# A decay-attention and gated-convolution kernel on one core: decay from ln(a_re), two small first units, a column-tiled state product and a pinned order

## The chip, the core and the metric

The kernel runs on one core of a Trainium2 chip. A core has five engines that work side by side and wait for one another through semaphores: TensorE (PE in the profile; its weight loads are shown apart as PEld), VectorE (DVE), ScalarE (ACT), GpSimd (POOL) and SyncE (SP), which here issues every DMA. The metric is the device time of one execution in microseconds. Three executions of the kernel before are shown, with their median; the profile is of one more execution.

## What is computed

For each of 4 batches and 8 heads, a state of 48 x 48 complex numbers decays by a complex factor per row and step, takes in an outer product of k and v, and is read out with q. The outputs of the 8 heads, side by side (384 columns), then go through a gated convolution. The reference, cut:

```
mag = np.sqrt(a_re * a_re + a_im * a_im)
scale = np.minimum(mag, 0.999) / (mag + 1e-06)
a_re_n, a_im_n = (a_re * scale, a_im * scale)
for t in range(S):                                  # S = 768
    new_re = ar * S_re - ai * S_im                  # ar, ai: step t of a_re_n, a_im_n
    new_im = ar * S_im + ai * S_re
    S_re, S_im = (new_re + kv, new_im)              # kv: outer product of k[t], v[t]
    y[:, :, t] = np.einsum('bhd,bhde->bhe', q[:, :, t], S_re)
...
gate = 1.0 / (1.0 + np.exp(-gate_pre))              # gate_pre: 5 taps along the sequence
return (gate * (x @ w_val) @ w_out)                 # x: y with the heads side by side
```

All inputs but the three convolution weights are float32; those are float64 and are rebuilt as float32 from their 64-bit words on the core.

## The kernel before

The recurrence is turned into chunked attention. The running product of the decay factors has a logarithm (a running sum of log magnitudes) and an angle (a running sum of angles). k is multiplied by one over that product and q by the product, each as a cosine and a sine part, so a head has 96 rows (48 cosine, 48 sine). The sequence is cut into 6 chunks of 128 steps. A chunk's output is a masked score matrix times v plus q times the state left by the chunks before.

The work goes in units: (batch, first head, number of heads). There are seven units of 4 heads and, at the end, two of 2 heads. A unit passes through these stages; a letter names each in the string `ORDER`:

- A, X, R (lines 277 to 360): from `ar` and `ai` to the running sums. ACT squares both inputs (L277, L279), takes one logarithm of both squares (L294, 2304 elements a partition), two exponentials (L296, L298), and the arctangent (L312). Two further ACT passes, L315 and L321, are guards: a Relu whose sum is not zero where an input lies outside the range that the formulas hold for. DVE does L281, L301, L316, the running sums along a partition (L244) and the shifts that fold the angle into one turn. PE adds the sums of the partitions below (L251, tile `off`).
- S (L368, L372): sine and cosine. E (L377, L379): the two exponentials of the log magnitude, each with a sum that the guard tests too.
- B (L391, L394): `kx` and `qx` (the latter in the tile `trig`). `kx` is also written to DRAM (`kd`) and read back with the sequence along the partitions (`kn`).
- T (L436, L437): transposes on PE, one head at a time, copied by ACT out of PSUM into `kq` (96 partitions x 768 steps, for k and q).
- s, k (L459, L464): scores of a chunk on PE, masked by DVE into `sm`. t (L495, L500): the state product `kn` (stationary, 96 columns) times `v` (48 columns), summed up in PSUM and copied by ACT to `S_sb`. y (L477, L480, L481): the chunk's output. The outputs of odd heads go to PSUM partitions 64 and up, those of even heads to partition 0 and up.
- W: the convolution's weights. C (L521, L524): the taps on DVE. G (L532): the sigmoid on ACT. M (L539, L545, L571, L576): the two projections on PE, the gating product on DVE, the copy and the store of the output.

`ORDER` is walked letter by letter; each letter lets one stage issue its next step. A framework then places the instructions of an engine, with one restriction that the kernel adds (`in_turn`): ACT instructions that need a table set keep their order. Loads and stores on SP are issued as soon as their buffers are free by the program's own count.

A float32 matmul is two instructions on PE (a transpose is one), each with its weight load.

Of the kernel before, what the change touches and what calls it, by code (L numbers as in the profile page):

```python
# [10 lines left out]
F32 = mybir.dt.float32  # L11
U32 = mybir.dt.uint32
I64 = mybir.dt.int64
I32 = mybir.dt.int32
# [8 lines left out]
    "WWAWWWAWWWWAXXXXRRRRRRRRRWRRWRRWRRWRWRRWRSSEEBWBWWWWBWWWBTTTTWWWWWWWWWWsksyWksWAAAXXXWtXWyWksRWt"  # L23
    "WRyWksWRWtRWyWksRWtWRWykRWWtRWyCCRCCRtCRCARRARSSEEBBBAXXXXRRRRRRRRRRRRRRBTTTTtsksykskysktysSSEEB"
    "ktBBBysktyTtyTTtTACsksAkstCyAXXXXRRRRRRRRRRRRRCRSSEEBkstCAyCAkstCCCyAXXBCXCkstXyCCGMMMMMMMMMMMMM"
    "ktyBtyRRRRRRMRRRMBTTTTtstksyksytRkRMRRMsRSSyMtMkMMsyMtMkMMsCyEMtkCyAAAXXXEBBBBCXRRRRRRRRRRRRRRCT"
    "TCTSTttskskysytkytsksAytSEACCCCCCCCCCCksCAXyCGMMMMMMMMtEBMMBMMMXkyXXBRRRMRRMRRMRMRBTTTTstksykyst"
    "RMRRMRksMRSSEEyMtMAMksMyMtACCBMCCCCksAXytXkBytXBXRRRRRRRRRBTTTTsttkskysksyksRAAtAXXXXRyksRtRCCCy"
    "kCCRSSECCCCCCCGCCCCCCMMMMMMMMMMMMMtRREBBBRRRyRBTRRRRtRTtsksRMRMRMMMMMMMyCCCCCtkCMsMyktMMsyktsykt"
    "SSEEBBBBTsyktyTskstyyksytksytksytksytkytCCCCCCCCCCCCGCCCCCCGCCCCCCGMMMMMMMMMMMMMMMMMMMMMMMMMM"  # L30
)
TURN = 2.0 ** 24
# [3 lines left out]
SS_MIN = 0.25  # L36
RHO_MAX = 1.5
RE_MIN = 0.75
SS_MAX = 1.8
# [3 lines left out]
def kernel(  # L43
# [50 lines left out]
    last = [None]  # L94

    def in_turn(ins):

        if last[0] is not None:
            tc.add_manual_dep(
                ins.ins, last[0].name,  # L100
                mybir.DependencyInfo(mybir.DependencyClass.NoSync, mybir.DependencyReason.DATA),
                reason="one table set after the other",
            )
        last[0] = ins.ins
        return ins

    loaded = [None]

    def table_set(name):
        if loaded[0] != name:  # L110
            in_turn(nc.scalar.preload_act_table_set(name))  # L111
            loaded[0] = name
# [3 lines left out]
    def load(u, nm):  # L116
        b, h0, g = units[u]
        tl = tiles.setdefault(u, {"v": []})
        if nm == "v":
            for hn in range(2):  # L120
                vt = ld.tile([C, HN, g, D], F32, name="v_in", bufs=VB)
                for h in range(g):
                    nc.sync.dma_start(
                        out=vt[:, :, h, :],
                        in_=v[b, h0 + h, hn * HS:(hn + 1) * HS].rearrange("(n i) e -> i n e", i=C),
                    )
                tl["v"].append(vt)
        else:
            t = ld.tile([P, 2, g, JH, D], F32, name=f"{nm}_in", tag="in")
            for f in range(2):  # L130
                nc.sync.dma_start(  # L131
                    out=t[:, f].rearrange("p h j d -> p h (j d)"),
                    in_={"ar": a_re, "ai": a_im, "k": k, "q": q}[nm][b, h0:h0 + g, f * HS:(f + 1) * HS].rearrange(
                        "h (p j) d -> p h (j d)", j=JH
                    ),
                )
            tl[nm] = t
# [9 lines left out]
    load(0, "ai")  # L147

# [17 lines left out]
    b_tiny = const.tile([P, 1], F32, name="b_tiny")  # L166
    nc.gpsimd.memset(b_tiny, 2.0 ** -60)
    b_re = const.tile([P, 1], F32, name="b_re")
    nc.gpsimd.memset(b_re, RE_MIN)
    b_ss = const.tile([P, 1], F32, name="b_ss")  # L170
    nc.gpsimd.memset(b_ss, -math.log(SS_MAX))
    over = const.tile([P, 4, NU], F32, name="over")
    flag = const.tile([1, 1], I32, name="flag")
    junk = const.tile([P, G * D * J], BF16, name="junk")
# [4 lines left out]
    b_rho = const.tile([P, 1], F32, name="b_rho")  # L179
    nc.gpsimd.memset(b_rho, math.log(2.0 ** 31 / RHO_MAX))  # L180

# [72 lines left out]
    tmps = []  # L254

# [8 lines left out]
    def new_tmp(ne):  # L264
        tmps.append(False)
        return work.tile([P, 2, ne], F32, name="tmp", bufs=TMPB), len(tmps) - 1

    def tmp_free():
        return len(tmps) < TMPB or tmps[-TMPB]

    def prep_a(u):

        b, h0, g = units[u]
        tl = tiles[u]
        tl["main"] = work.tile([P, 2, JH, 2, g * D], F32, name="main", bufs=MAINB)
        main, mf, mj = views(u)
        nc.scalar.activation(mj[:, 1], jm(tl["ar"]), AF.Square)  # L277
        yield
        nc.scalar.activation(mj[:, 0], jm(tl["ai"]), AF.Square)  # L279
        yield  # L280
        nc.vector.scalar_tensor_tensor(  # L281
            out=mf[:, 0], in0=mf[:, 1], scalar=SS_MIN, in1=mf[:, 0], op0=ALU.max, op1=ALU.add
        )

    def prep_x(u):

        b, h0, g = units[u]
        tl = tiles[u]
        main, mf, mj = views(u)
        while not tmp_free():  # L290
            yield "wait"
# [663 lines left out]
```

## Time and profile before

| | us |
|---|---|
| median of three executions | 351.21 |
| lowest, highest of the three | 350.67, 356.26 |
| the profiled execution | 352.57 |
| its span, first to last instruction | 350.9 |
| PE busy / DVE busy / ACT busy in the span | 291.3 / 254.8 / 266.7 |
| DMA share of the 16 engines | 53.2% |

Busy time is the time that records of an engine cover. Matmul records overlap: one lasts about 0.25 us, the next may start 0.1 us after it. So how long PE needs for a row of matmuls is read from the distance of their starts, and not from their mean duration. The granted TensorE clock was 0.992 over the span.

### The profile page before, as it was taken

The page shows a single profiled execution, that of the slowest core. Times are in us where ns is not written, and L with a number is a line of the kernel's source. Part 1 is how long each engine was busy: PE and PEld are TensorE (multiplying, and loading weights), DVE is VectorE, ACT ScalarE, POOL GpSimd, SP SyncE. Part 2 cuts the span into 40 slices and gives each one's busy share as a digit, 9 for nine tenths or more (in the row PEclk, how much of TensorE's full clock was granted, in tenths as well). Part 3 has the DMA queues.
Part 4 walks back from the last instruction along what each step waited for, and adds up shares of the span by engine and source line. Part 5 has one row for each costly group of instructions (what it writes and reads, how often), then busy time and mean ns, then how long its engine had stood idle before and what let it go on. Part 6 is the DMA issues. An engine that isn't in the chain of part 4 may idle for free.

```text
span 350.9 us, 5801 instructions
## 1 busy us (share of the span) xinstructions
PE 291.3 (83%) x2154; PEld 221.7 (63%) x2154; DVE 254.8 (73%) x322; ACT 266.7 (76%) x454; POOL 2.5 (1%) x23
## 2 busy tenths in 40 slices
PE   0030298958988998999999999999999999999992
PEld 0020187748767775777887767777877775676551
DVE  0599987899685998788989786788479736356610
ACT  3958989998998989599879986998996375362201
POOL 2000000000000000000000000000000000000000
PEclk9999999989999999999999999999999999999998
DMA  7993781269579549745674576458410532520102
GB/s 230 370 243 67 241 239 61 61 196 356 124 214 256 148 117 296 220 110 174 194 210 102 151 218 212 95 186 275 92 39 2 153 102 92 164 48 21 62 32 67
DMA packets 84562, 54.73 MB, mean 156 GB/s; under 512 B 31024, under 2 KB 83760, under 8 KB 84528
## 3 DMA queue, kind: packets, MB, share of 16 engines
q1 hardware_dynamic: 84528, 54.30, 53.2%
q8 instruction: 19, 0.31, 0.4%
q14 instruction: 15, 0.12, 0.1%
HBM read 35.40 MB, written 14.16 MB: 141 GB/s over the span
## 4 chain that ended last, share of the span: by engine, by line
PE 67%; ACT 14%; DVE 6%; DMA 5%; SPq 3%; issue 2%; ACTq 0%
PE pv L539 13%; PE po L571 12%; PE pt L436 11%; PE sc L459 10%; PE S_ps L495 7%; PE y_ps L477 5%; PE y_ps L480 5%; PE off L251 3%; SPq L131 2%; DMA q_in<-in_q_dram 2%; ACT main L294 2%; ACT L111 2%; DMA kn<-kd 1%; ACT kq L437 1%; ACT junk L315 1%
## 5 line engine op out<-in xcount | busy, mean ns | idle before, releaser
L437 ACT COPY kq<-pt 96x384 f32<-96x384 f32 x128 | 55.8, 478 | 6.6 <-PE pt L436 6.1
L459 PE MATMUL sc<-kq 96*128 96x128 f32 x384 | 58.3, 282 | 2.0 <-DVE sm L464 2.0
L459 PEld LDWEIGHTS sc<-kq 96*128 96x128 f32 x384 | 50.6, 193 | 10.5 <-DVE sm L464 4.8
L539 PE MATMUL pv<-xT,wv_sb 128*128 128x384 f32 x144 | 54.8, 498 | 0.0
L571 PE MATMUL po<-wo_sb,z 128*128 128x384 f32 x144 | 51.7, 496 | 1.0 <-DVE z L545 1.0
L464 DVE TENSOR_TENSOR sm<-sc,mask 128x512 f32<-128x512 f32 (+1 forms) x54 | 34.0, 629 | 25.5 <-PE sc L459 15.7
L524 DVE SCALAR_TENSOR_TENSOR z<-xT,cw_sb,z 128x768 f32<-128x768 f32 (+1 forms) x60 | 50.6, 854 | 1.1
L436 PE MATMUL pt<-ident,kx 128*96 128x128 f32 x192 | 34.0, 288 | 15.1 <-DVE kx L394 12.2
L477 PE MATMUL y_ps<-kq,S_sb 96*48 96x128 f32 x320 | 39.8, 286 | 3.9 <-ACT y_sb L481 3.0
L480 PE MATMUL y_ps<-sm,v_in 128*48 128x128 f32 x384 | 42.1, 275 | 0.1
L436 PE MATMUL pt<-ident,trig 128*96 128x128 f32 x192 | 34.0, 286 | 6.4 <-DVE trig L394 5.0
L495 PE MATMUL S_ps<-v_in,kn 128*96 128x48 f32 x320 | 36.8, 247 | 1.3 <-DMA kn<-kd 0.8
L495 PEld LDWEIGHTS S_ps<-v_in,kn 128*96 128x96 f32 x320 | 34.0, 167 | 6.0 <-issue 4.5
L571 PEld LDWEIGHTS po<-wo_sb,z 128*128 128x128 f32 x144 | 25.7, 190 | 17.1 <-DVE z L545 2.3
L436 PEld LDWEIGHTS pt<-ident,kx 128*96 128x96 f32 x192 | 21.5, 132 | 21.7 <-DVE kx L394 12.9
L111 ACT ACT_TABLE_LOAD x25 | 32.1, 1283 | 1.2 <-PEq L939 0.8
L481 ACT COPY y_sb<-y_ps 112x256 f32<-112x256 f32 (+1 forms) x54 | 18.6, 345 | 18.2 <-PE y_ps L480 17.8
L436 PEld LDWEIGHTS pt<-ident,trig 128*96 128x96 f32 x192 | 21.7, 132 | 16.1 <-issue 6.9
L539 PEld LDWEIGHTS pv<-xT,wv_sb 128*128 128x128 f32 x144 | 24.4, 190 | 9.9 <-issue 0.9
L576 ACT COPY ot<-po 128x384 f32<-128x384 f32 x24 | 11.4, 478 | 24.1 <-PE po L571 23.8
L477 PEld LDWEIGHTS y_ps<-kq,S_sb 96*48 96x48 f32 x320 | 21.1, 122 | 13.6 <-ACT y_sb L481 5.6
L480 PEld LDWEIGHTS y_ps<-sm,v_in 128*48 128x48 f32 x384 | 27.4, 123 | 3.1 <-issue 0.7
(81 smaller groups left out, 394.5 us busy)
## 6 DMA issues: line engine op xcount, KB each, us to landing
kd<-kx SPq DMA_DIRECT2D x14, 576.0 KB, 3.5
kn<-kd SPq DMA_DIRECT2D x14, 576.0 KB, 4.7
v_in<-in_v_dram SPq DMA_DIRECT2D x64, 72.0 KB, 2.7
out_dram<-ot SPq DMA_DIRECT2D x24, 192.0 KB, 2.3
ar_in<-in_a_re_dram SPq DMA_DIRECT2D x14, 288.0 KB, 4.0
ai_in<-in_a_im_dram SPq DMA_DIRECT2D x14, 288.0 KB, 4.8
k_in<-in_k_dram SPq DMA_DIRECT2D x14, 288.0 KB, 3.4
q_in<-in_q_dram SPq DMA_DIRECT2D x14, 288.0 KB, 4.6
```

The lines of the kernel that those rows point to most:

```text
L111: in_turn(nc.scalar.preload_act_table_set(name))
L436: nc.tensor.transpose(pt[:C2, j, :], src[:, j, f, h, :], ident)
L437: nc.scalar.copy(tj[:, s, f], pt[:C2].rearrange("c j p -> c p j"))
L459: nc.tensor.matmul(sc[:, h, :], self.part(0, h, n), self.part(1, h, n), start=True, stop=True)
L464: nc.vector.tensor_tensor(out=sm, in0=sc[:, :g], in1=mask[:, None, :].to_broadcast([C, g, C]), op=ALU.mult)
L477: nc.tensor.matmul(o, self.S_sb[n - 1][:, h * D:(h + 1) * D], self.part(1, h, n), start=True, stop=False)
L480: nc.tensor.matmul(o, vt[:, h, :], sm[:, h, :], start=(n == 0), stop=True)
L481: nc.scalar.copy(self.y_sb[:112, :, (n % HN) * C:(n % HN + 1) * C], yp[:112, :g // 2 * C].rearrange("e (r t) -> e r t", t=C),)
L495: nc.tensor.matmul(self.S_ps[:C2, h * D:(h + 1) * D], kn[:, h, :], vt[:, h, :], start=(n == 0 and h == 0), stop=(n == NCH - 2), skip_group ...
L524: nc.vector.scalar_tensor_tensor(out=z, in0=xT[:, c, EXT + t0 - t:EXT + t0 - t + n], scalar=cw_sb[:, TAPS - 1 - t, c:c + 1], in1=z, op0=AL ...
L539: nc.tensor.matmul(pv[:, :n], wv_sb[:, ci, c * P:(c + 1) * P], xT[:, ci, EXT + t0:EXT + t0 + n], start=(ci == 0), stop=(ci == NT - 1),)
L571: nc.tensor.matmul(po[:, :DM], z[ci][:, m:m + P], wo_sb[:, ci, :], start=(ci == 0), stop=(ci == NT - 1))
```

## The change

The change does five things.

1. The decay. With l = ln(a_re) and t = a_im / a_re, the log of the squared magnitude is 2 l + ln(1 + t^2), and the angle is arctan(t). ACT now does: logarithm, exponential, square, logarithm, exponential, arctangent, all on 1152 elements for a unit of four heads. The two Relu passes go; the sum that the guard needs comes along with the square (`accum_out`). DVE has three full passes as before.
2. The first unit of four heads is cut into two units of two heads. There are now 10 units: 2, 2, six of 4, 2, 2.
3. The state product of a head is two matmuls, of 64 and of 32 stationary columns. Their outputs lie at PSUM partitions 0 to 63 and 64 to 95, in different column tiles of PE.
4. X, R and A have one stream for even and one for odd units (upper and lower case letters), so that two units' preparation can be interleaved. Loads (L, V), the read-back (N), the collection of outputs (D) and the stores (O) become steps of `ORDER` too, and `ORDER` is new throughout.
5. Each instruction on PE, ACT, DVE and SP is tied to the one written before it on its engine, so that the order written is the order run.

The diff, cut to its core:

```diff
-    "WWAWWWAWWWWAXXXXRRRRRRRRRWRRWRRWRRWRWRRWRSSEEBWBWWWWBWWWBTTTTWWWWWWWWWWsksyWksWAAAXXXWtXWyWksRWt"
...
+    "XXLLLXLXXXxxXXRxRRRWWARRLWAWWxRSWLLSAEEWWWWWWWBLXBVWXBxXWBLVxWTXXXTTVxxTWWWXrXRTNtNrTWrRrTrTtsar"
...
-    units = [(b, h0, G) for b in range(B) for h0 in range(0, H, G)][:-1] + [(B - 1, H - G, 2), (B - 1, H - 2, 2)]
+    units = [(0, 0, 2), (0, 2, 2)] + [(b, h0, G) for b in range(B) for h0 in range(0, H, G)][1:-1]
+    units += [(B - 1, H - G, 2), (B - 1, H - 2, 2)]
...
-        nc.scalar.activation(mj[:, 1], jm(tl["ar"]), AF.Square)
-        nc.scalar.activation(mj[:, 0], jm(tl["ai"]), AF.Square)
...
-        in_turn(nc.scalar.activation(mf, mf, AF.Ln, bias=b_tiny))
-        in_turn(nc.scalar.activation(tmp[:, 1], mf[:, 1], AF.Exp, bias=b_rho, scale=-0.5))
-        in_turn(nc.scalar.activation(tmp[:, 0], mf[:, 0], AF.Exp, bias=b_inv, scale=-0.5))
...
-        nc.scalar.activation(junk[:, :ne], mf[:, 0], AF.Relu, bias=b_ss, accum_out=over[:, 1, u:u + 1])
...
+        nc.scalar.activation(mj[:, 0], jm(tl["ar"]), AF.Ln)
+        nc.scalar.activation(tmp, mf[:, 0], AF.Exp, scale=-1.0)
...
+        nc.scalar.activation(tmp, mf[:, 1], AF.Square, accum_out=over[:, 0, u:u + 1])
+        nc.scalar.activation(tmp, tmp, AF.Ln, bias=b_one)
+        nc.vector.scalar_tensor_tensor(out=mf[:, 0], in0=mf[:, 0], scalar=2.0, in1=tmp, op0=ALU.mult, op1=ALU.add)
+        nc.scalar.activation(tmp, mf[:, 0], AF.Exp, bias=b_inv, scale=-0.5)
...
-                nc.tensor.matmul(
-                    self.S_ps[:C2, h * D:(h + 1) * D], kn[:, h, :], vt[:, h, :],
-                    start=(n == 0 and h == 0), stop=(n == NCH - 2), skip_group_check=True,
-                )
+                for c0, c1 in ((0, 64), (64, C2)):
+                    nc.tensor.matmul(
+                        self.S_ps[c0:c1, h * D:(h + 1) * D], kn[:, h, c0:c1], vt[:, h, :],
+                        start=(n == 0 and h == 0), stop=(n == NCH - 2), skip_group_check=True,
+                    )
...
+    for ins in nc.cur_bb.bb.instructions:
+        if ins.engine not in IN_ORDER:
+            continue
+        if ins.engine in before:
+            tc.add_manual_dep(
+                ins, before[ins.engine].name,
...
+                reason="the order that the steps are written in",
```

The built programs show where this moves instructions. First the start of ACT's queue, before the change (`ar_in`, `ai_in` are inputs, `main` and `tmp` the work tiles, `cvt` belongs to the weights):

```order
L111 ACT_TABLE_LOAD
L277 ACTIVATE main<-ar_in 128x1152
L279 ACTIVATE main<-ai_in 128x1152
L277 ACTIVATE main<-ar_in 128x1152
L294 ACTIVATE main<-main,b_tiny 128x2304
L279 ACTIVATE main<-ai_in 128x1152
L296 ACTIVATE tmp<-main,b_rho 128x1152
L298 ACTIVATE tmp<-main,b_inv 128x1152
L111 ACT_TABLE_LOAD
L315 ACTIVATE junk,over<-main,b_ss 128x1152
L312 ACTIVATE main<-main 128x1152
```

And the same place after it:

```order
L99 ACT_TABLE_LOAD
L253 ACTIVATE main<-ar_in 128x576
L257 ACTIVATE tmp<-main 128x576
L264 ACTIVATE tmp,over<-main 128x576
L267 ACTIVATE tmp<-tmp,b_one 128x576
L253 ACTIVATE main<-ar_in 128x576
L257 ACTIVATE tmp<-main 128x576
L272 ACTIVATE tmp<-main,b_inv 128x576
L99 ACT_TABLE_LOAD
L287 ACTIVATE main<-main 128x576
```

Every pass now has half the elements, the Relu between the table load and the arctangent is gone, and two passes of the second unit stand where the first unit waits for DVE.

Next DVE's queue around the first `kx`, for which PE's first transposes wait, before:

```order
L202 TENSOR_SCALAR cvt<-cvt 128x384
L193 TENSOR_SCALAR cvt<-raw 128x384
L391 TENSOR_TENSOR main<-main,k_in 128x1152
L215 SCALAR_TENSOR_TENSOR wv_sb<-cvt,wv_sb 128x384
L394 TENSOR_TENSOR kx<-trig,main 128x2304
L391 TENSOR_TENSOR main<-main,q_in 128x1152
L215 SCALAR_TENSOR_TENSOR wo_sb<-cvt,wo_sb 128x384
L394 TENSOR_TENSOR trig<-trig,main 128x2304
```

and after:

```order
L188 SCALAR_TENSOR_TENSOR wv_sb<-raw,cvt 128x384
L192 TENSOR_TENSOR wv_sb<-wv_sb,cvt 128x384
L354 TENSOR_TENSOR main<-main,k_in 128x576
L357 TENSOR_TENSOR kx<-trig,main 128x1152
L197 SCALAR_TENSOR_TENSOR wv_sb<-cvt,wv_sb 128x384
L354 TENSOR_TENSOR main<-main,q_in 128x576
L259 TENSOR_TENSOR main<-tmp,ai_in 128x1152
L175 TENSOR_SCALAR cvt<-raw 128x384
L357 TENSOR_TENSOR trig<-trig,main 128x1152
```

The products of the first unit are half as long, and a full pass of the third unit (L259) now stands between them.

Last, PE in the middle of the run, at a state product beside an output, before:

```order
L495 MATMUL S_ps<-v_in,kn 96x48
L571 MATMUL po<-wo_sb,z 128x384 x2
L459 MATMUL sc<-kq 128x128 x4
L477 MATMUL y_ps_131<-kq,S_sb 48x128
L480 MATMUL y_ps_131<-sm,v_in 48x128
L477 MATMUL y_ps_131<-kq,S_sb 48x128
L480 MATMUL y_ps_131<-sm,v_in 48x128
L477 MATMUL y_ps_131<-kq,S_sb 48x128
L480 MATMUL y_ps_131<-sm,v_in 48x128
L477 MATMUL y_ps_131<-kq,S_sb 48x128
L480 MATMUL y_ps_131<-sm,v_in 48x128
L436 MATMUL pt<-ident,kx 96x128 x3
```

and after:

```order
L401 MATMUL pt<-ident,trig 96x128 x3
L461 MATMUL S_ps<-v_in,kn 64x48
L461 MATMUL S_ps<-v_in,kn 32x48
L461 MATMUL S_ps<-v_in,kn 64x48
L461 MATMUL S_ps<-v_in,kn 32x48
L461 MATMUL S_ps<-v_in,kn 64x48
L461 MATMUL S_ps<-v_in,kn 32x48
L461 MATMUL S_ps<-v_in,kn 64x48
L461 MATMUL S_ps<-v_in,kn 32x48
L443 MATMUL y_ps_130<-kq,S_sb 48x128
L446 MATMUL y_ps_130<-sm,v_in 48x128
L443 MATMUL y_ps_130<-kq,S_sb 48x128
```

A state product now alternates between outputs of 64 and of 32 partitions, four heads in a row, and stands directly ahead of an output of 48 partitions. In the whole program a state product stands next to an output product at 25 places before and at 36 after. The built program gives each matmul a tile width: 128 columns for all but `y_ps` (64) before; after it, the two halves of a state product have 64 and 32.

More of the change, by code (lines that the diff above doesn't have):

```diff
@@ L165 @@
     )
[L166 to L172, printed above, removed]
+    b_one = const.tile([P, 1], F32, name="b_one")
+    nc.gpsimd.memset(b_one, 1.0)
+    over = const.tile([P, 3, NU], F32, name="over")
     flag = const.tile([1, 1], I32, name="flag")
-    junk = const.tile([P, G * D * J], BF16, name="junk")
     b_quart = const.tile([P, 1], F32, name="b_quart")
@@ L337, in prep_r @@
         )
-        yield
-        if u < BOTH:
-            yield from add_up(main[:, 0])
-        off = offset(main[:, 0], dmat, gd)
         yield
@@ L353, in prep_r, with prep_a @@
         )
+    def prep_a(u):
+        b, h0, g = units[u]
+        gd = g * D
+        main, mf, mj = views(u)
+        off = offset(main[:, 0], dmat, gd)
         yield
@@ new lines, with move @@
+    for u in range(2, NU):
+        order += [(u, nm) for nm in ("ar", "ai", "k", "q")]
+    order = [(0, "ar"), (0, "ai"), (1, "ar"), (1, "ai")] + order
+    for x in order[:4]:
+        done[("L",) + x] = True
+    at["L"] = 4
+    halves_of = [(u, hn) for u in range(NU) for hn in range(2)]
+    outs = []
+    def move(key):
+        i = at[key]
+        if key == "L":
+            if i >= len(order) + 2:
+                return False
+            if i in (WL, WL + 1):
+                load_raw((w_val, w_out)[i - WL])
+            else:
+                j = i if i < WL else i - 2
+                if j >= LB and not done.get(order[j - LB][::-1]):
+                    return False
+                load(*order[j])
+                done[("L",) + order[j]] = True
+        elif key == "O":
+            if i >= len(outs):
+                return False
+            b, m, ot = outs[i]
+            nc.sync.dma_start(out=out[b, m:m + P], in_=ot)
+        else:
+            if i >= len(halves_of):
+                return False
+            u, hn = halves_of[i]
+            if key == "V":
+                if u not in tiles or i >= VB and not done.get(("y",) + chunks[HN * (i - VB) + HN - 1]):
+                    return False
+                load_v(u, hn)
+            elif key == "N":
+                if not done.get(("kd", u)) or i >= KNB and at["t"] < HN * (i - KNB + 1) - (i - KNB) % 2:
+                    return False
+                load_kn(u, hn)
+            else:
+                if not done.get(("y", u, HN * hn + HN - 1)) or not room_for_x(units[u][0]):
+                    return False
+                att[u].collect(hn)
+            done[key, u, hn] = True
+        at[key] += 1
+        return True
```

319 lines of the change are left out of this document (137 added, 182 removed).

## The prediction

> **What bounds the kernel now.** I read the rows by slice first, then four stretches, then the chain of work that ended last, then the timeline of PE at its start, and last the groups of one shape for durations. By slice, PE (tenths of 40 equal slices) is nearly empty for five slices and nearly full after the twelfth:
>
> ```profile
> PE   0030298958988998999999999999999999999992
> ...
> PE 67%; ACT 14%; DVE 6%; DMA 5%; SPq 3%; issue 2%; ACTq 0%
> ```
>
> The second line is the chain's share by engine: PE carries two thirds of it. Four stretches (us; busy time of PE, PEld, DVE, ACT, POOL; clock, DMA):
>
> ```profile
> 0.00:45.00 45.00, 5.79 (x20) 4.43 (x21) 32.73 (x51) 33.49 (x37) 2.22 (x20) 1.00 0.79 231
> 45.00:110.00 65.00, 54.73 (x495) 47.01 (x494) 52.14 (x57) 61.16 (x105) 0.11 (x1) 0.97 0.62 182
> 110.00:345.00 235.00, 230.76 (x1643) 170.31 (x1641) 169.93 (x215) 172.08 (x314) 0.21 (x2) 1.00 0.48 137
> 345.00:351.00 6.00, 0.00 (x0) 0.00 (x0) 0.00 (x0) 0.00 (x0) 0.00 (x0) 0.83 0.12 38
> ```
>
> From 110 us on PE is the bound: 230.8 of 235. From 45 to 110 ACT is (61.2 of 65), and PE loses 10.3. To 45 the chain of the first unit is, and PE loses 39.2. The timeline of PE (start, length, gap before and what ended it) shows where that begins, and ACT's last copy where PE ends:
>
> ```profile
> 37.99 0.87 PE L436 MATMUL pt<-ident,kx 128*96 128x128 f32 x3 [11.92 <-DVE kx L394]
> ...
> 344.43 0.48 ACT L576 COPY ot<-po 128x384 f32<-128x384 f32 x1 [1.46 <-PE po L571]
> ```
>
> **What PE's own work takes.** Distances of starts, from the timeline and the chain:
>
> ```profile
> 108.62 0.85 PE L495 MATMUL S_ps<-v_in,kn 128*96 128x48 f32 x8 [0.76 <-DMA kn<-kd]
> 109.31 0.56 PE L251 MATMUL off<-main,dturn 128*128 128x192 f32 x2
> ...
> 263.99 1.06 PE L459 MATMUL sc<-kq 96*128 96x128 f32 x8
> 264.98 0.64 PE L480 MATMUL y_ps<-sm,v_in 128*48 128x128 f32 x8
> ...
> 268.24 0.38 PE L480 MATMUL y_ps<-sm,v_in 128*48 128x128 f32 x2
> 268.55 0.91 PE L571 MATMUL po<-wo_sb,z 128*128 128x384 f32 x2
> ...
> 114.53 0.66 PE pt L436 x6
> ...
> 214.90 1.30 PE off L251 x8
> ...
> 332.74 5.80 PE pv L539 x18
> ...
> L459 PE MATMUL sc<-kq 96*128 96x128 f32 x384 | 58.3, 282 | 2.0 <-DVE sm L464 2.0
> L495 PE MATMUL S_ps<-v_in,kn 128*96 128x48 f32 x320 | 36.8, 247 | 1.3 <-DMA kn<-kd 0.8 <-ACT S_sb L500 0.6
> L480 PE MATMUL y_ps<-sm,v_in 128*48 128x128 f32 x384 | 42.1, 275 | 0.1
> ```
>
> `S_ps`: (109.31 - 108.62) / 8 = 0.086 us an instruction. `sc`: (1.06 - 0.28) / 7 = 0.111. `y_ps`: (0.64 - 0.275) / 7 = 0.052, half of `sc` for the same 128 moving columns, so two heads in two column tiles run side by side. `pt` 0.11, `off` 0.163, `pv` and `po` 0.322. A change of tile width costs: the last `sc` of eight starts at 263.99 + 0.78 = 264.77 and `y_ps` 0.21 later, not 0.11; the last `y_ps` starts at 268.24 + 0.38 - 0.275 = 268.35 and `po` 0.20 later. About 0.1 us each way.
>
> Instructions (two for a matmul, one for a transpose): `sc` 384 x 0.111 = 42.6, `pt` 384 x 0.11 = 42.2, `pv` and `po` 288 x 0.322 = 92.7, `y_ps` 704 x 0.052 = 36.6, `S_ps` 320 x 0.086 = 27.5, `off` 72, 16 of them half as long, 10.4: together 252.0. The order before has 130 changes of width: 13.0. PE ends at 344.4: 252.0 + 13.0 + 38.0 before the first transposes leaves 41.4 of waits and small gaps after that.
>
> **The change, part by part.**
>
> *Start.* Durations of half-size passes, which the two last units have already:
>
> ```profile
> L111 ACT ACT_TABLE_LOAD x25 | 32.1, 1283 | 1.2 <-PEq L939 0.8
> ...
> L244 DVE TENSOR_TENSOR main<-main 128x384 f32<-128x384 f32 x8 | 4.2, 553 | 0.1
> ...
> L394 DVE TENSOR_TENSOR kx<-trig,main 128x1152 f32<-128x1152 f32 x2 | 2.7, 1347 | 0.0
> ...
> L315 ACT ACTIVATION_READ_ACCUMULATOR junk<-main,b_ss 128x1 f32 x9 | 1.7, 189 | 0.0
> ...
> L296 ACT ACTIVATE tmp<-main,b_rho 128x576 f32<-128x576 f32 x2 | 1.6, 786 | 0.0
> ...
> L301 DVE TENSOR_TENSOR main<-tmp,ai_in 128x576 int32<-128x576 f32 x2 | 1.5, 754 | 0.4 <-ACT tmp L296 0.4
> ...
> L277 ACT ACTIVATE main<-ar_in 128x576 f32<-128x576 f32 x2 | 1.4, 696 | 0.0
> ...
> L347 DVE TENSOR_SCALAR main<-main 128x576 uint32<-128x576 uint32 x2 | 0.9, 450 | 0.0
> ```
>
> The first input reached ACT at 4.91 us; half the bytes take less to land (medians below), so 3.6.
>
> ```profile
> 4.91 1.16 ACT L277 ACTIVATE main<-ar_in 128x1152 f32<-128x1152 f32 x1 [2.81 <-DMA ar_in<-in_a_re_dram]
> ...
> ar_in<-in_a_re_dram SPq DMA_DIRECT2D x14, 288.0 KB, 4.0
> ...
> ar_in<-in_a_re_dram SPq DMA_DIRECT2D x4, 144.0 KB, 2.7
> ```
>
> The chain to `kx`, in the order shown: ACT six passes without a bias tile (Ln, Exp, Square, Arctan, Abs, Sin) and one exponential, 7 x 0.70 = 4.9; three with one, 3 x 0.79 = 2.4; two passes of the second unit in between, 0.6 of them not beside DVE; two table loads 2.6; two accumulator reads 0.4; one weight pass 0.5. DVE: four passes of 0.75, one shift of 0.45, two sums of 0.55, `kx` 1.35: 5.9. PE's `off` with its hops, by estimate, 0.9. Together 18.2; overlaps of neighbours and hops between engines I set against each other. So `kx` is there at 3.6 + 18.2 = 21.8 and PE begins 16.2 us earlier. The bounds are 19 (every pass overlaps the next by a tenth of a us or more) and 24 (four weight passes of 0.55 on DVE fall on the chain).
>
> *The first units bring half as much.* A unit of four heads holds 252.0 - 92.7 = 159.3 / 8, or 20 us of PE; the first now 10. Its successor's products come after more DVE work than that, so PE runs dry for up to 10 us. I take 10. In the pinned order the first state product also stands ahead of the last transposes of the second head and waits for `kn`, which comes back one write and one read after `kx`:
>
> ```profile
> kd<-kx SPq DMA_DIRECT2D x4, 288.0 KB, 2.8
> kn<-kd SPq DMA_DIRECT2D x4, 288.0 KB, 3.7
> ```
>
> That is 6.5 us, or 28.3, when the transposes ahead of it have just ended (the q product is there at about 26); what it costs is in the 10.
>
> *Decay.* For a full unit:
>
> ```profile
> L294 ACT ACTIVATE main<-main,b_tiny 128x2304 f32<-128x2304 f32 x7 | 15.5, 2217 | 0.0
> ...
> L315 ACT ACTIVATE junk<-main,b_ss 128x1152 bf16<-128x1152 f32 x7 | 8.8, 1253 | 0.0
> ...
> L279 ACT ACTIVATE main<-ai_in 128x1152 f32<-128x1152 f32 x7 | 8.1, 1161 | 2.1 <-DMA ai_in<-in_a_im_dram 2.1
> ```
>
> Out go one Square (1.16), the long Ln (2.22), two Relus (2.5) and two reads (0.4); in come two Ln (1.16 and 1.25) and one read (0.2): 3.7 us less ACT a unit, 29 in all, less some 4 for cutting one more unit in two (ten passes at 2 x 0.70 against 1.16, and more small copies) and 2.6 for two more table loads (30 against 28). After 110 us ACT waits for PE, and this is worth little there. From 45 to 110 ACT is the bound, and about three units pass: up to 11. I take 10, which cancels the 10 above. The bounds for both and for the pinned order together are 15 better (nothing runs dry, 4.2 us of PE's idle time after 110 go too) and 15 worse (nothing gained, and in-order queues add 5). DVE's passes stay; SP issues the same loads, and an early `kn` read queues behind loads of `k` and `v`, which is in the 15.
>
> *State product in two column tiles.* PE's time here is the weight load: 0.086 us for 96 columns, 0.0009 a column, while 48 moving columns need less. Mean weight loads agree:
>
> ```profile
> L495 PEld LDWEIGHTS S_ps<-v_in,kn 128*96 128x96 f32 x320 | 34.0, 167 | 6.0 <-issue 4.5 <-ACT S_sb L500 0.9
> ...
> L480 PEld LDWEIGHTS y_ps<-sm,v_in 128*48 128x48 f32 x384 | 27.4, 123 | 3.1 <-issue 0.7 <-DVE sm L464 0.3
> ```
>
> (167 - 123) / 48 is 0.92 ns a column. If the two tiles load and run side by side as `y_ps` does, a head costs two loads of 64 columns, 0.115 us, where it cost 0.172: 160 heads and chunks x 0.057 = 9.1 saved. If they don't, 96 columns in all cost what they did: 0. Changes between 128 and a narrower width go from 130 to 146: 1.6 more. No row shows a change from 64 to 32 columns; by the nearest, 128 to 64, it would cost 0.1, by two tiles of one width nothing. I take nothing, since the two halves occupy different columns, as the two tiles of `y_ps` do and a 128-wide matmul and `y_ps` do not.
>
> The Trainium skill, page "TensorEngine Tiling (Array Packing)", section "Tiling Modes", says that changing the tiling mode, and not just the tile, drains TensorE, and lists 128x64 and 128x32 as different configurations. The trace agrees for 128 against 64 (0.1 us); for 64 against 32 no run here shows it yet. By it the result is that of the first rival below, and by the row of `y_ps` alone the sum below.
>
> *Sum.* Stream 252.0 - 9.1 = 242.9 (more small `off` for fewer large ones change nothing); changes of width 14.6; start 21.8; other waits 41.4; end after PE 350.9 - 344.4 = 6.5: 327.2. The profiled execution took 352.57, 1.7 over its span and 1.4 over the median, so on the scale of the median this is 0.3 more, or 328. Its own bounds: 16 to 18 either way, 311 to 345.
>
> **Rivals.**
>
> *Slower: each change between 64 and 32 drains PE.* A head alternates widths, and I count 297 such changes. At 0.1 us: 29.7. The halves then follow each other: the 32-wide one adds 2 x 0.04 for its 48 moving columns (0.322 / 384 each), 12.8 in all. A quarter lies where PE waits anyway, so 5 are hidden: 328 + 29.7 + 12.8 - 5 = 366. It decides the sign from 0.03 us a change on ((351 - 328 - 12.8) / 297). For it: the 0.1 between 128 and 64; against it: `y_ps` shows disjoint columns at work together.
>
> *The early start is given back.* PE starts at 21.8, but two short units need DVE and ACT for as many passes as two long ones, so that the later units come no earlier than before: 328 + 16 = 344. For it: ACT 61.2 of 65; against it: ACT's 3.7 us less a unit.
>
> *The two tiles don't overlap.* The state product does not do what its form says: 328 + 9 = 337.
>
> **How the numbers follow.** My forecast, 328, has 0.58; the given-back start (344, half of it within 2%) 0.16; tiles without overlap (337) 0.08; draining (366) 0.18. About 2%, 344 to 358, is what a measurement of this kernel can tell from no change. Faster: 0.56 + 0.08 + 0.07 = 0.71; within: 0.02 + 0.09 + 0.05 = 0.16; slower 0.13. From 311 to 358 all but about 0.19 is held: the tail under 311 and most of the draining.
>
> **What would show it.** First transposes at 19 to 24; ACT busy near 245; `S_ps` pairs whose 32-wide half starts within 0.03 us of a 64-wide one, against 0.15 or more if PE drains; 243 us of stream by the same distances. The forecast is wrong if PE still idles 80 us in all, or if the state product's share of the chain grows.

## The result, and the profile after

| | before | after |
|---|---|---|
| median of the runs beside each other | 351.73 us (350.67 to 356.26, 4 runs) | 388.23 us (386.44 to 388.52, 4 runs) |
| ratio, with its 95% interval | | 1.104 (1.100 to 1.109) |
| profiled execution: time, span | 352.57, 350.9 us | 386.44, 384.7 us |

The changed kernel is slower by a tenth; the forecast was 328 us, and 311 to 358 as its range. The kernel before was timed again with each group of experiments, on the chip that ran them; its medians there were 350.7 to 355.6, so ratios and not microseconds compare runs of different groups.

The page of the changed kernel, PE and its granted clock by slice (9.6 us each), and the chain of work that ended last, by engine:

```profile
PE   0217897897999999999999999999999999999995
...
PEclk9999959579999999999999999999999999999999
...
PE 76%; ACT 9%; DMA 6%; SPq 3%; DVE 3%; issue 2%; DVEq 0%; ACTq 0%
```

PE's part of the chain rises from 67 to 76%, that of the state product alone from 7 to 17%. The early start is there (the first slices are less empty), and the sixth, eighth and ninth slices have a clock of 0.5 to 0.7 that the kernel before did not have. The groups that answer to the state product, the copy behind it and the table loads:

```profile
L461 PE MATMUL S_ps<-v_in,kn 128*32 128x48 f32 (+1 forms) x640 | 77.0, 233 | 2.8 <-DMA kn<-kd 2.8
...
L466 ACT COPY S_sb<-S_ps 96x192 f32<-96x192 f32 (+1 forms) x50 | 14.1, 282 | 49.2 <-PE S_ps L461 49.2
...
L99 ACT ACT_TABLE_LOAD x30 | 38.5, 1283 | 1.3 <-PEq L945 0.8
```

The state product's busy time has doubled (36.8 before), and ACT waits 49 us for it, in front of the copy. The stretches:

```profile
45.00:110.00 65.00, 56.42 (x409) 42.83 (x411) 53.79 (x69) 53.91 (x95) 0.11 (x1) 0.82 0.67 176
110.00:345.00 235.00, 233.96 (x1845) 174.89 (x1845) 158.40 (x191) 153.00 (x285) 0.22 (x2) 1.00 0.49 136
345.00:386.00 41.00, 34.98 (x165) 20.76 (x163) 15.80 (x30) 10.01 (x24) 0.00 (x0) 0.99 0.15 50
```

From 110 us PE is busy without a break, as before (234.0 of 235), but it now needs 35 us more. From 45 to 110 ACT is no longer full (53.9 of 65, where it was 61.2), and PE, on a clock of 0.82, does less than before: 409 instructions against 495. The timeline of PE at the start, and one state product of four heads in the steady part:

```profile
24.62 0.87 PE L401 MATMUL pt<-ident,kx 128*96 128x128 f32 x3 [9.63 <-DVE kx L357]
28.65 0.85 PE L401 MATMUL pt<-ident,trig 128*96 128x128 f32 x3 [3.16 <-DVE trig L357]
29.29 0.85 PE L401 MATMUL pt<-ident,kx 128*96 128x128 f32 x3
...
166.86 1.86 PE L461 MATMUL S_ps<-v_in,kn 128*64 128x48 f32 x16
168.65 0.53 PE L401 MATMUL pt<-ident,trig 128*96 128x128 f32 x3
```

First transposes at 24.6 (38.0 before, 21.8 forecast). Three transposes take 29.29 - 28.65 = 0.64 us, twice the 0.33 that the same three take in the steady part: PE starts at half speed. The clock row doesn't show this, since its first record is at 44.2 us (48.6 in the kernel before); the 1.00 of the stretches ahead of that is no reading, and the 0.992 over the span doesn't count it. Up to that record PE's starts stand twice as far apart as behind it in both kernels, 0.21 us for transposes: from 38.0 to 48.6 before, from 24.6 to 44.1 after. So the early start is 20 us at half speed, where 10.6 stood before. And a state product of four heads lasts 168.65 - 166.86 = 1.79 us; before it was 109.31 - 108.62 = 0.69, and the forecast was 0.46. With 160 heads and chunks, 40 such groups, that is 44 us more.

### The profile page after: what moved, and what is told of

The parts are those of the page before. It is cut to its first block, busy times and chain, and to the rows that moved or that the text cites. A ratio compares the mean times of both kernels' runs of the same rounds, so it can differ in the third digit from the quotient of the medians.

```text
span 384.7 us, 6464 instructions
## 1 busy us (share of the span) xinstructions
PE 341.3 (89%) x2482; PEld 251.1 (65%) x2482; DVE 258.7 (67%) x338; ACT 250.3 (65%) x454; POOL 2.5 (1%) x20
## 4 chain that ended last, share of the span: by engine, by line
PE 76%; ACT 9%; DMA 6%; SPq 3%; DVE 3%; issue 2%; DVEq 0%; ACTq 0%
PE S_ps L461 17%; PE pv L505 12%; PE po L537 12%; PE pt L401 11%; PE sc L425 11%; PE y_ps L443 5%; PE y_ps L446 5%; DMA raw<-in_moe_w_out_dram 3%; PE off L233 3%; ACT kq L402 2%; ACT L99 2%; SPq L109 2%; DMA ai_in<-in_a_im_dram 1%; DMA kn<-kd 1%; ACT main L287 1%
## 5 line engine op out<-in xcount | busy, mean ns | idle before, releaser
L461 PE MATMUL S_ps<-v_in,kn 128*32 128x48 f32 (+1 forms) x640 | 77.0, 233 | 2.8 <-DMA kn<-kd 2.8
L461 PEld LDWEIGHTS S_ps<-v_in,kn 128*32 128x32 f32 (+1 forms) x640 | 54.6, 124 | 28.4 <-issue 6.6
L505 PE MATMUL pv<-xT,wv_sb 128*128 128x384 f32 x144 | 49.5, 488 | 0.0
L466 ACT COPY S_sb<-S_ps 96x192 f32<-96x192 f32 (+1 forms) x50 | 14.1, 282 | 49.2 <-PE S_ps L461 49.2
L401 PE MATMUL pt<-ident,kx 128*96 128x128 f32 x192 | 36.1, 302 | 10.6 <-DVE kx L357 9.9
L401 PE MATMUL pt<-ident,trig 128*96 128x128 f32 x192 | 36.1, 301 | 4.7 <-DVE trig L357 4.3
L443 PE MATMUL y_ps<-kq,S_sb 96*48 96x128 f32 x320 | 36.9, 292 | 3.4 <-ACT y_sb L447 3.4
L505 PEld LDWEIGHTS pv<-xT,wv_sb 128*128 128x128 f32 x144 | 26.1, 190 | 15.2 <-issue 0.4
L401 PEld LDWEIGHTS pt<-ident,kx 128*96 128x96 f32 x192 | 22.7, 138 | 17.8 <-DVE kx L357 10.4
L446 PEld LDWEIGHTS y_ps<-sm,v_in 128*48 128x48 f32 x384 | 25.1, 126 | 7.0 <-DVE sm L430 4.8
L401 PEld LDWEIGHTS pt<-ident,trig 128*96 128x96 f32 x192 | 22.2, 136 | 10.8 <-ACT tmp L264 3.6
L443 PEld LDWEIGHTS y_ps<-kq,S_sb 96*48 96x48 f32 x320 | 18.2, 123 | 10.4 <-ACT y_sb L447 4.5
```

The lines of the kernel that those rows point to most:

```text
L401: nc.tensor.transpose(pt[:C2, j, :], src[:, j, f, h, :], ident)
L443: nc.tensor.matmul(o, self.S_sb[n - 1][:, h * D:(h + 1) * D], self.part(1, h, n), start=True, stop=False)
L446: nc.tensor.matmul(o, vt[:, h, :], sm[:, h, :], start=(n == 0), stop=True)
L461: nc.tensor.matmul(self.S_ps[c0:c1, h * D:(h + 1) * D], kn[:, h, c0:c1], vt[:, h, :], start=(n == 0 and h == 0), stop=(n == NCH - 2), skip ...
L505: nc.tensor.matmul(pv[:, :n], wv_sb[:, ci, c * P:(c + 1) * P], xT[:, ci, EXT + t0:EXT + t0 + n], start=(ci == 0), stop=(ci == NT - 1),)
```

## The experiments

Theory D is the first rival of the prediction: each change between 64 and 32 columns holds PE up. The others are named in the expectations. All ratios are to the kernel before.

**The state product whole again, the rest of the change kept.**

```diff
-                for c0, c1 in ((0, 64), (64, C2)):
-                    nc.tensor.matmul(self.S_ps[c0:c1, ...], kn[:, h, c0:c1], vt[:, h, :], ...)
+                nc.tensor.matmul(self.S_ps[:C2, ...], kn[:, h, :], vt[:, h, :], ...)
```

> The changed kernel with the state product whole again (one matmul of 96 columns a head). Theory D (each change between 64 and 32 columns drains PE): the profile after shows 0.447 us for a head's state product where 0.172 stood before; 160 x 0.275 = 44 us go away again, so 388 - 44 = 344, and between 334 and 346 if the colder clock of the first 82 us improves too. Theory O (the pinned order and the small first units cost it, the state product little): over 370.

Measured: 352.03 us (351.66 to 355.09), ratio 1.005 (0.999 to 1.011). So the split costs 36 us, and the order and the rest (theory O) do not. But 352 is not 344 either: without the split the change gains nothing, which opens a second question. The timeline of PE in this run has the state product as it was:

```profile
158.56 0.88 PE L460 MATMUL S_ps<-v_in,kn 128*96 128x48 f32 x8
159.28 0.50 PE L401 MATMUL pt<-ident,trig 128*96 128x128 f32 x3
```

159.28 - 158.56 = 0.72 us for four heads, against 1.79.

**The split alone, in the kernel before.** The same edit the other way round.

> The kernel before with only the state product split into 64 and 32 columns. Theory D: 352 + 44 = 396, 388 to 398 (a part falls where PE waits anyway). Theory O: the split alone costs little, under 362.

Measured: 394.49 us (391.94 to 397.95), ratio 1.122 (1.114 to 1.129), as D expected. Nothing pins the order there, and the compiler's scheduler put rows of PE, DVE and ACT elsewhere as well, so not all of the 44 us need be PE's own. A run further down, with equal tiles in the same kernel, narrows it to 35.

**All halves of 64 of a chunk first, then all of 32.** The same instructions and loads, one change of width a chunk instead of one a head.

```diff
-            for h in range(self.g):
-                for c0, c1 in ((0, 64), (64, C2)):
+            for c0, c1 in ((0, 64), (64, C2)):
+                for h in range(self.g):
```

> The changed kernel with the 64-wide matmuls of all heads of a chunk first and then the 32-wide ones: one change of width inside a chunk in place of seven. Theory D: four heads cost 4 x 0.115 + 0.15 + 4 x 0.09 = about 1.0 us where they now cost 4 x 0.447 = 1.79; 40 such chunks give 32 us: 356. Theory L (two narrow weight loads instead of one cost the time, in whatever order): 386 to 390.

Measured: 362.52 us (360.3 to 363.88), ratio 1.032 (1.026 to 1.039). The timeline of PE:

```profile
166.81 1.12 PE L461 MATMUL S_ps<-v_in,kn 128*64 128x48 f32 x16
167.86 0.65 PE L446 MATMUL y_ps<-sm,v_in 128*48 128x128 f32 x8
```

1.05 us for four heads instead of 1.79: 40 x 0.74 = 30 us less, of which 26 show. The number of instructions and loads is the same, so the order of widths is what costs. In the single records, away from a change, starts lie 0.058 us apart from 64 to 64 and 0.043 from 32 to 32: 8 x 0.058 + 8 x 0.043 = 0.81. So of the 0.59 over the forecast 0.46, 0.35 is that halves of one width and one column tile follow each other and don't overlap, and 0.24 is the changes at the middle and at the end.

**Two tiles of one width.** The second half takes 64 columns too, its last 32 being the next head's (which nobody reads); `kn` gets 32 more columns for the last head, zeroed on POOL.

```diff
-                for c0, c1 in ((0, 64), (64, C2)):
+                for c0, c1 in ((0, 64), (64, 128)):
...
-                        self.S_ps[c0:c1, h * D:(h + 1) * D], kn[:, h, c0:c1], vt[:, h, :],
+                        self.S_ps[c0:c1, h * D:(h + 1) * D], kn[:, h * C2 + c0:h * C2 + c1], vt[:, h, :],
```

> The changed kernel with both halves of the state product 64 columns wide: the second takes in 32 columns of the next head, whose results (PSUM partitions 96 to 127) nothing reads. No change of width inside a chunk. Theory D: as with the outputs, the two tiles run side by side; a head costs two loads of 64 columns, 0.115 us; 388 - 160 x 0.33 = 335. Theory L: two loads of 64 columns one after the other are 0.23 us a head: 388 - 35 = 353; theory O: over 370.

Measured: 349.89 us (349.03 to 351.46), ratio 0.997 (0.992 to 1.003). The timeline of PE:

```profile
168.06 0.67 PE L463 MATMUL S_ps<-v_in,kn 128*64 128x48 f32 x16
168.56 0.61 PE L447 MATMUL y_ps<-sm,v_in 128*48 128x128 f32 x8
```

0.50 us for four heads, 0.125 a head with what lies between groups: the two tiles run side by side, as the forecast had it for 64 and 32. But the time stays 15 over the 335 expected. By the time alone theory L's 353 fits better; its 0.23 us a head is ruled out by the timeline. Against the whole product PE saves 160 x 0.055 = 9 us here, and the time falls by 2, within the noise.

**The second question, the clock.** In the run with equal tiles PE was at half clock from 47.3 to 57.6 and from 64.4 to 78.0, and three times later for 3.4; before only from 75.9 to 79.3. (Stretches in these two runs last 3.4, 10.2 or 13.6 us.) With the half speed ahead of the first record, from the first transposes on, that is 54 us against 14. The next run fills PE's longest waits up to 72 us with transposes of the identity that nobody reads.

```diff
+    warm = {"pt0": 36, "pt1": 12, "S0": 12, "y0": 8, "y1": 4, "pt8": 2, "pt9": 4, "pt16": 6, "y5": 10, "pt17": 5, "y6": 4}
...
+        for _ in range(warm.get(f"{kind}{seen[kind]}", 0)):
+            nc.tensor.transpose(y_ps[0][:, 384:512] if dst is None else dst, ident, ident)
```

> The kernel with two equal column tiles of 64 (349.9), and 103 transposes of the identity into PSUM columns that nothing reads, put on PE ahead of the instructions at which it waited longest up to 72 us; nothing of the result is left out. Theory C (the clock: PE starts early but with gaps, runs at half clock for some 46 us against some 14 before, and loses the early start to that): the half-clock time falls below 25 us, PE's products come 8 to 10 us sooner, and the time is 341 (338 to 344). Theory P (the order: the work that PE waits for comes no sooner, since ACT, DVE and the load queue work through a fixed list): the half-clock time falls too, but PE waits longer instead, and the time is 349 (347 to 352).

Measured: 345.47 us (343.77 to 348.12), ratio 0.982 (0.975 to 0.990): about half of what theory C expected, and the fastest whole kernel of this study. The clock by slice (some 8.7 us each), first with equal tiles, then warmed, and the stretch from 45 to 110 us of both:

```profile
PEclk9999977659899989899999999999999999999998
```

```profile
PEclk9996999998999997899999999999999999999998
```

```profile
45.00:110.00 65.00, 54.55 (x486) 44.36 (x486) 55.63 (x72) 58.34 (x102) 0.86 (x7) 0.79 0.69 185
```

```profile
45.00:110.00 65.00, 55.92 (x580) 44.31 (x582) 60.54 (x75) 62.47 (x115) 0.73 (x6) 0.97 0.82 217
```

The clock rises from 0.79 to 0.97 and DVE and ACT get more done in the same time. From the first k transposes on, PE is at half clock for 17 us instead of 54. So 37 us of half clock are worth about 5 here (0.015 of 351). By that price the 17 left would be worth some 2 more, by estimate; the rest of the gap is not the clock.

**The load queue.** SP's order is left free; PE, ACT and DVE stay pinned. In the run with equal tiles the chain of work goes through it (start, length):

```profile
123.13 0.58 SPq L367
...
123.75 0.63 SPq L367
...
124.43 1.23 SPq L109
...
125.70 6.98 DMA ar_in<-in_a_re_dram
```

L367 is the write of `kd`, which waits for `kx`; the next unit's load (L109) stands behind it.

> The kernel with two equal column tiles of 64 (349.9), with SP's queue of transfers taken out of the list of engines whose order is pinned; PE, ACT, DVE and POOL stand exactly as they did. Theory P in its narrow form (the inputs of later units are issued behind a write that waits for DVE, as at 123 to 131 us, and that is what gives the early start back): the loads move ahead of it, the waits of ACT for ar_in fall from 7.1 us to under 3, and the time is 343 (339 to 346). If the queue is not the cause (theory C, or the pinned order of ACT and DVE): 349 (346 to 353), with the waits moved to other places.

Measured: 349.92 us (348.45 to 351.38), ratio 0.994 (0.988 to 1.000). ACT's waits for `ar_in` fell only from 7.1 to 5.0 us, where under 3 was expected, and PE's wait in front of the projection that this chain feeds was as long as before (2.8 us there, 3.1 here). Freeing the queue's order does not change the time.

**Two parts alone, in the kernel before.** Equal tiles alone, and the decay part alone (the five new ACT passes, no Relu).

> The kernel before with one edit: the state product in two column tiles of 64 each, the second running into 32 columns of the next head that nothing reads (a padded kn, one POOL fill of 32 columns per half). By the distances of the run with equal tiles a head costs 0.115 us instead of 0.172, 9.1 us of PE in all, and PE is the bound from 110 us on: 343 (340 to 346). If PE's time is not what sets the end of the kernel before (waits take the place of the saving): 350 (348 to 352).

> The kernel before with the decay part alone: ln(a_re), the tangent from exp(-ln), no Relu passes, one guard sum in the place of two; units, state product and order of steps as before. My prediction took 10 us for it, from about three units at 3.7 us less of ACT between 45 and 110 us: 341 (338 to 344). Against it: the new chain goes from ACT to DVE and back twice where the old one went once, about 2 us more to the first kx, and after 110 us ACT waits for PE anyway: 351 (349 to 355).

Measured: 359.47 us (357.93 to 361.91), ratio 1.022 (1.015 to 1.029), and 372.67 (369.88 to 380.8), ratio 1.056 (1.049 to 1.064). Neither theory expected that, and neither run is a clean test of its part: in the kernel before the scheduler orders the steps by its own estimates, and with each edit it chose another order. That the order costs more than the edits bring is a reading and not shown: no run holds this order and changes the edit.

One comparison is clean, or nearly. Equal tiles and the split of 64 and 32, each alone in this kernel, gave the same order of DVE (322 of 322 rows) and ACT (418 of 418), and of PE but for some ten rows. They differ in the width of the second half: 359.47 against 394.49, 35 us by the ratios (1.122 / 1.022). So the cost of the unequal widths stands without the pinned order too.

**The pin.** So the next run takes the pin away from the kernel with equal tiles.

```diff
-IN_ORDER = (mybir.EngineType.PE, mybir.EngineType.Activation, mybir.EngineType.DVE, mybir.EngineType.SP)
+IN_ORDER = ()
```

> The kernel with two equal column tiles of 64 (349.9), with no engine's order pinned: the compiler's scheduler orders the same steps by its own estimates. My prediction costed the pinned order at nothing by itself: 350 (346 to 354). If the pinned order is what holds the kernel back: under 344. If it is worth something, as the two edits of the kernel before suggest, which were slower under the free scheduler than forecast: over 356.

Measured: 372.28 us (371.9 to 373.93), ratio 1.061 (1.055 to 1.068). The pinned order is worth 22 us against what the scheduler makes of the same program, so leaving it to the scheduler is no way to the missing time. Whether another pinned order is better stays open.

**More and less work on ACT and DVE, order kept.** Three runs on the warmed kernel. Two Relu passes a unit put back as bare load:

> The warmed kernel with equal tiles (345.5), with ACT's two guard passes put back as bare load: two Relu passes and their two accumulator reads after each unit's Arctan, on a constant, with results that nobody reads; 2.9 us of ACT for a full unit, 24 in all. By the decay term of my prediction (ACT is the bound from 45 to 110 us, some three units pass there, and about 10 us hang on it) the time rises by 8 to 10, to 354. If ACT isn't what sets the pace there (DVE is, at 60.5 of 65 us): 347 (345 to 349).

Measured: 367.19 us (365.98 to 368.14), ratio 1.045 (1.038 to 1.052): 22 more, for passes of

```profile
L299 ACT ACTIVATE junk<-mask,b_one 128x1152 bf16<-128x1152 f32 (+1 forms) x20 | 21.1, 1056 | 0.3
```

and 3.7 us of accumulator reads; ACT's busy time rose by 21.5. Where the time comes in is read from the k products on DVE, the fourth unit's and the last one's. Warmed, then with the load:

```profile
90.59 2.55 DVE L365 TENSOR_TENSOR kx<-trig,main 128x2304 f32<-128x2304 f32 x1
...
284.27 1.35 DVE L365 TENSOR_TENSOR kx<-trig,main 128x1152 f32<-128x1152 f32 x1
```

```profile
105.56 2.55 DVE L372 TENSOR_TENSOR kx<-trig,main 128x2304 f32<-128x2304 f32 x1
...
304.95 1.35 DVE L372 TENSOR_TENSOR kx<-trig,main 128x1152 f32<-128x1152 f32 x1
```

The same product is 15.0 us later at 105, and 20.7 at the end. Most of the price falls before 110 us. Not all of it is ACT's: PE's clock is colder too. This is the stretch that had 0.97 in the warmed kernel:

```profile
45.00:110.00 65.00, 51.29 (x454) 41.47 (x453) 52.75 (x70) 58.27 (x102) 0.73 (x6) 0.87 0.56 155
```

From the first k transposes on PE is at half clock for 37.5 us instead of 17, in part perhaps since the transposes that fill the waits no longer stand where the waits are. At 5 us for 37 that is some 3 of the 22, by estimate.

The weight conversion left out (DVE's busy time falls by 15.5 us, from 257.8 to 242.3; the projections use a constant in the place of the weights):

> The warmed kernel with equal tiles (345.5), with the conversion of the two weight matrices and the taps left out (POOL fills them with a constant instead), so that 17 us of DVE and 3 of ACT go out of the first 110 us; all other steps stand as they did. Theory S (supply: from 24 to 110 us DVE is the bound, 80.9 of 86 us, so whatever the early start gains on PE is given back to it): products come up to 17 us sooner by 110 us and the time is 334 (330 to 338). If other waits (transfers, ACT, the order) take its place: 343 to 346.

Measured: 342.96 us (341.47 to 345.66), ratio 0.975 (0.969 to 0.982): 2.5 less than the warmed kernel, which is within the noise, and not 11. Theory S falls. The first k product ended at 22.1 instead of 24.0.

Two ACT passes a unit left out; ACT's busy time falls by 17.8 us (the square of the tangent and the logarithm behind it are missing, so the decay's magnitude is another):

> The warmed kernel with equal tiles (345.5), with two of ACT's ten preparation passes of a unit left out, the square of the tangent and the logarithm behind it (the magnitude of the decay is then wrong): 2.6 us of ACT for a full unit, 21 in all, all of it before 270 us. Theory A (ACT is the bound until some 110 us, 62.5 of 65 us busy, and each us there counts): 13 to 18 us go, 330 (326 to 334). Theory F (the fixed order: it fits the durations that it was made for, so added work is passed on in full, as the 24 us that cost 22, while work removed leaves holes in front of the same waits): 343 (340 to 346).

Measured: 344.78 us (341.9 to 345.6), ratio 0.978 (0.971 to 0.986): 0.7 less. Theory F fits: 21.5 us more of ACT's busy time cost 22, the clock's share in it, and 17.8 us less give nothing that can be measured. One run each way does not show that the fixed order is the reason.

**The second unit.** With the state product whole, the k products of the changed kernel on DVE begin at

```profile
22.47 1.36 DVE L357 TENSOR_TENSOR kx<-trig,main 128x1152 f32<-128x1152 f32 x1
...
46.99 1.35 DVE L357 TENSOR_TENSOR kx<-trig,main 128x1152 f32<-128x1152 f32 x1
...
59.62 2.56 DVE L357 TENSOR_TENSOR kx<-trig,main 128x2304 f32<-128x2304 f32 x1
...
95.59 2.55 DVE L357 TENSOR_TENSOR kx<-trig,main 128x2304 f32<-128x2304 f32 x1
...
290.64 1.35 DVE L357 TENSOR_TENSOR kx<-trig,main 128x1152 f32<-128x1152 f32 x1
```

and those of the kernel before at

```profile
35.39 2.55 DVE L394 TENSOR_TENSOR kx<-trig,main 128x2304 f32<-128x2304 f32 x1
...
64.22 2.55 DVE L394 TENSOR_TENSOR kx<-trig,main 128x2304 f32<-128x2304 f32 x1
...
94.02 2.55 DVE L394 TENSOR_TENSOR kx<-trig,main 128x2304 f32<-128x2304 f32 x1
...
291.78 1.35 DVE L394 TENSOR_TENSOR kx<-trig,main 128x1152 f32<-128x1152 f32 x1
```

Two heads are ready 14 us earlier (23.8 against 37.9), but the third and fourth 10 us later (48.3 against 37.9), the next four 5 us earlier, the next four 1.6 us later, and the last two hardly earlier. A count of PE's work says where the lead goes. With each instruction that has started priced by the distances of the prediction, PE had done 7.0 us of its 252 by 45 us (2.6 in the kernel before), 10.8 by 55 (10.3), 14.9 by 65 (17.2) and 44.5 by 110 (45.6). The lead is gone by 55 us, when the second unit is just ready, though in that stretch the clock is at half too, from 46.4 to 56.6. Two runs therefore put the second unit's remaining passes ahead of the third's in the first 130 or 145 letters of the table (on the warmed kernel; the rest of the table unchanged).

> The warmed kernel with equal tiles (345.5), with the table of steps changed in its first 130 letters only: the second unit's remaining ACT and DVE passes stand ahead of the third unit's long ones (both streams, same passes, same number of table loads). Theory U (the start is given back by the second unit, whose k product came at 46.7 us here, where the kernel before had all four heads' at 37.9): it comes at 39 to 42, PE has done 3 to 6 us more by 60 us, and the time falls by as much, to 341 (338 to 343). If the third unit and the later ones set the pace whatever the second does (their k products at 59.2 and 93.1): 345 (343 to 347).

Measured: 354.62 us (353.37 to 357.33), ratio 1.007 (1.004 to 1.011). The timeline of PE shows a fault of the edit:

```profile
49.71 1.62 PE L241 MATMUL off<-main,dturn 128*128 128x192 f32 x4 [12.64 <-DVE main L234]
```

The third unit's `off` product stood ahead of the second unit's transposes and held PE 12.6 us. The k products of the second and the third unit on DVE:

```profile
41.13 1.36 DVE L365 TENSOR_TENSOR kx<-trig,main 128x1152 f32<-128x1152 f32 x1
...
66.82 2.56 DVE L365 TENSOR_TENSOR kx<-trig,main 128x2304 f32<-128x2304 f32 x1
```

The second comes 4.2 us sooner than in the warmed kernel (it ended at 46.7 there), the third 10.2 later (59.2 there).

> The run before this one again, with its fault taken out: there PE stood 12.8 us (36.8 to 49.6) at the third unit's off product, which my edit had left ahead of the second unit's transposes in PE's order. Now off stands behind them, and DVE makes the second unit's two products before it goes on with the third. Theory U (the late second unit gives the start back): the second k product comes at 40 to 43 instead of 46.7, PE has done 3 to 5 us more by 60 us, and the time is 341 (338 to 343) against 345.5 for the warmed kernel. If what is gained at the second unit is lost at the third (its k product came at 59.2 and will come some us later): 347 (344 to 350).

Measured: 361.75 us (359.88 to 368.55), ratio 1.021 (1.010 to 1.032). Slower still. The second product is there at 44.4, 2.3 us sooner than in the warmed kernel, but the third at 77.9, 18.6 later. The profile is of the longest execution, 368.55 us. PE now waits for the mask product `sm`, which stands on DVE behind passes of the third unit that wait for ACT.

```profile
54.12 0.67 PE L457 MATMUL y_ps<-sm,v_in 128*48 128x128 f32 x4 [12.60 <-DVE sm L440]
```

Neither run is the test that theory U asked for, since each brought a new wait, and a colder clock with it: from the first k transposes on 27 us at half clock in the first and over 50 in the profile of the second, against 17. That the late second unit eats the lead is read from the products above; that another order could keep it is not shown.

## Why the prediction was wrong

*The bound.* Right for the changed kernel: PE is busy for 219.0 of the 220 us from 110 to 330 (216.4 before). Without the unequal widths it holds less well: 212.9 with the whole product and 213.4 with equal tiles, whose 9 us less of PE brought 2.

*The step that failed: "No row shows a change from 64 to 32 columns; ... I take nothing".* I took the row of `y_ps`, two tiles of one width, for two tiles of two widths. The measured head is 1.79 / 4 = 0.45 us and not 0.115: 160 x 0.33 = 53 us of PE more than in the sum. Against equal tiles, which cost what the sum took, the time shows 38 of them; against the whole product, where PE's difference is 44, it shows 36. The rival named the mechanism, and the Trainium skill's sentence on it, that a change of tiling mode drains TensorE ("TensorEngine Tiling (Array Packing)", section "Tiling Modes"), agrees with these runs: with equal widths the pair overlaps, with 64 and 32 it doesn't and each change costs time, at the same count of instructions. In the single records of the changed kernel, starts lie 0.094 us apart from a 64-wide instruction to the next one of its matmul, 0.067 from 32 to 32, and 0.151 and 0.136 at the two changes, 0.448 a head. Away from any change, in the grouped run, the same halves in a row take 2 x 0.058 + 2 x 0.043 = 0.20. So the lost overlap is 0.09 a head over the 0.115, and a change costs (0.448 - 0.202) / 2 = 0.12, part of it at the instruction behind the change. The rival took 0.08 and 0.1 and was right in both to about a fifth. What it added to the forecast, 37.5, is close to the 388.2 - 349.9 = 38.3 measured against equal tiles. That is partly luck: PE's price was 53 and not 42.5, and 15 of it were hidden and not 5. Its 366 was too low because it stood on a 328 that the rest of the change did not reach. That I gave it 0.18 is the misjudgement: the only row for "a change of width costs" said 0.1 us, and the only row against it had no change of width in it.

*Start.* 21.8 forecast, with bounds 19 and 24; 24.6 measured, 2.8 too low and outside the bounds. The sum had one weight pass on the chain; without any of them the product came 1.9 us sooner. And it had 0.9 for PE's `off` with its hops, which takes 2.0 us, from 12.99 to the end at 14.98: its eight instructions start 0.21 us apart, where the same shape has 0.11 late in the run.

```profile
12.99 1.14 PE L233 MATMUL off<-main,dturn 128*128 128x96 f32 x4 [12.99 <-DVE main L226]
13.92 1.06 PE L233 MATMUL off<-main,dmat 128*128 128x96 f32 x4
```

*"I take 10, which cancels the 10 above": the first units run dry, and ACT's relief pays for it.* This is the second failed step. With the state product whole, PE's last matmul ends at about 345.7:

```profile
23.89 0.88 PE L401 MATMUL pt<-ident,kx 128*96 128x128 f32 x3 [8.85 <-DVE kx L357]
...
345.74 0.48 ACT L541 COPY ot<-po 128x384 f32<-128x384 f32 x1 [1.46 <-PE po L536]
```

345.7 - 23.9 (start) - 252.0 (stream) - 11.8 (118 changes of 128 against less) = 58.0 us of other waits, where the sum had 41.4. The bound that I gave for this ("15 worse") is about what happened. About 5 of the 17 are the clock, by the gain of the warmed run: the sum priced all of PE's work at full speed. For the other 12 the trace points to the second unit, whose product is 10.4 us later than that of all four heads was before; no run that moves it alone has shown it, so this stays a reading and the cause stays open. Either way the second rival (the early start given back) came true beside the first: with the whole product it reads 328 + 9 + 16 = 353, and 352 was measured.

*Decay.* ACT's busy time fell to 250.3 (forecast 245), with two more table loads, 30 against 28, as counted. That this brings 10 us is not shown by any run: 17.8 us less of ACT on the same order gave 0.7. Nor is it shown worthless: with 21.5 us more ACT the kernel is 22 slower. In this pinned order work added was paid and work removed was not. The decay part by itself remains untested, since in the kernel before the scheduler moved everything else with it.

*Signs named.* "Pairs start within 0.03 us, against 0.15 or more if PE drains" and "the state product's share of the chain grows" both came out against the forecast: the 32-wide half starts 0.15 us behind the last 64-wide one, and the share went from 7 to 17%.

## What to carry to other kernels

Two column tiles overlapped on PE when they had one width, and not as 64 and 32: pad the narrower one rather than alternate widths, and price any pair of shapes from a row that has that pair. (Padded tiles were not measurably faster here than the undivided product.) An earlier start is worth only what the following units can keep up: read when the second and third are ready, not the first. And read PE's speed there from the distances of its starts, since the clock row may begin later. A fixed order of all steps is best made again after an edit that changes durations: here it passed on what was added and gave nothing back for what was taken away, which no run has tried to mend with a new order.

## What was not expected of the hardware

A state product of four heads, sixteen instructions with the same moving data, takes 0.50 us with widths 64 and 64 (32 more stationary columns a head than the others), 1.05 with four of 64 and then four of 32, 1.79 with 64 and 32 in turn, and 0.72 as eight of 96.

PE's clock falls to half for stretches of 3.4 us or whole multiples of it, up to 23.9 in the slowest profile. In the 3.4 us ahead of the drops at 47.3 and 64.4 with equal tiles, PE's longest waits between short groups of matmuls were 1.6 and 1.5 us. The Trainium skill ("TensorE: Matmul & The Clock Gate", section "What's actually happening") gives an idle window of about 3.4 us; the lengths agree with it, but these drops came without a wait of that length. Transposes of the identity in the waits kept the clock up and gained 1.5%.
